# Two maxima over partitions: from a round through DRAM to a unit matrix and a matmul with ones, with a listed due for every planned step

## The chip, the cores and the metric

The kernel runs on one core of one Trainium2 chip. The metric is the device time of one execution in microseconds; of the kernel before, three runs gave 404.8, 405.76 and 405.9 us, so 405.76 us is the median. A profile was taken of one more execution.

## The reference, cut to what matters

```python
xn = layernorm(x)                                   # x: 2048 rows of 512
s  = irfft2(rfft2(xn) * (w_r + 1j * w_i))           # a global filter over rows and columns
gate, up = xn @ W_gate, xn @ W_up                   # 512 -> 1376
h  = gate * (gate > 0) * up
g  = silu(h @ W_down)                               # 1376 -> 512
out = x + s * g
```

All data are 32-bit floats. The kernel keeps that precision by splitting each operand into a high and a low half of 16 bits and adding three products (high by high, high by low, low by high). For that it has to know the size of the numbers: the columns of `W_down` are scaled by a power of two found from the greatest absolute value of the whole matrix, and the filter `w` by one found from the greatest sum of its squares. Each of these two maxima is first taken along the free axis, which leaves one number per partition in a column of 128, and then over the 128 partitions, with the result wanted in every partition. The second half of that is what the change touches.

## The kernel before, in words

The 2048 rows are worked on in eight chunks of two tiles of 128 rows (for the transform) and in four blocks of 512 rows (for the feed-forward part). A block's feed-forward work is eleven tiles of 128 hidden columns: `product` makes `gu` (gate and up) on TensorE, `rectify` makes `r` on ScalarE, `hidden` makes `h` on VectorE and splits it, `down` multiplies `h` by the scaled `W_down` into `dn`, and `gate` makes `g`. The last block does part of this with fewer products (`sa`, `sb`, `sc`). The transform is made of small matrix products: `first_stage` (`s` from `xs`, result `t` written to the DRAM tensor `A_d`), `fft_chunk` (`at` read back, then `y`, `xx`, the multiplication by the filter, `z`, `v`, written to `C_d`), `last_stage` (`ct` read back, `s` again, then `zz`, `ae`, `ye`, `sv` on ScalarE, VectorE and GpSimd), and `finish` (`sv` times `g`, plus `x`, written out).

Nothing of this is issued in the order in which the program states it. Each piece is a *step* with an engine, an estimated cost, the names it reads and writes, and perhaps a due time and a lead. `Plan.run` gives every step without a due time one from those that depend on it (lines 144 to 148), then simulates the engines: at each turn it takes, for each engine, the steps that could begin soonest (dependences met, a buffer free, not before due minus lead), among them the one with the smallest due (lines 191 to 196), and writes the instructions in that order. Every engine then runs its own list in order and waits by semaphores. Buffers come from pools with few places (`ROOM`, line 56: ten of `k4`, two of `F`, three of `gu` and one of `dn` in PSUM); a step that needs a new buffer follows the last reader of the old one. All loads and stores but the accumulating ones are issued by SyncE, in one queue.

`greatest(name, col, reads, due)` (line 728) takes the column over the partitions: SyncE writes it to a DRAM row of 128 numbers (4 bytes from each partition), reads that row back into all partitions as a 128x128 tile, and VectorE reduces it. It is called by `down_scale` (name `md`; its result leads to `scd`, which the scaled `W_down` tiles `wds` wait for) and by `filter_scale` (name `mw`; it leads to `cw` and `cwi`, used in `fft_chunk` and `last_stage`). In a profile all instructions have line 87, that of the helper through which they are issued; tiles tell them apart. `unit` (line 289) is the unit matrix and `ones` (line 306) a 128x128 matrix of ones, both there already for the transposes and for sums over partitions.

Of the kernel before, what the change touches and what calls it, by code (L numbers as in the profile page):

```python
# [8 lines left out]
F32 = mybir.dt.float32  # L9
I32 = mybir.dt.int32  # L10
AF = mybir.ActivationFunctionType
ALU = mybir.AluOpType
AX = mybir.AxisListType

P = 128
S, D, F = 2048, 512, 1376
# [45 lines left out]
TICK, TICK_TO = 1.158, 60  # L62
PLAINS = ['plain', 'plain', 'plain', 'plain', 'plain', 'plain', 'plain', 'plain', 'plain', 'plain', 'plain', 'plain', 'plain', 'plain', 'plain', 'fast', 'plain', 'fast', 'fast', 'fast']
XDUE, SDUE = [-18.3, 7.83, 88.22, 100.36, 188.84, 115.24, 195.7, 156.37], [-84.52, 3.8, 95.3, 188.33]


RANGES = ((0, 257, 0), (257, 512, 1))
# [7 lines left out]
def fwidth(f):  # L75
    return P if f < TAIL else F - P * TAIL
# [17 lines left out]
class Plan:  # L94
# [28 lines left out]
    def step(self, engine, cost, fn, reads=(), writes=(), due=None, lead=None, port=False, kb=0, margin=0., lag=None, mode=0, block=0.):  # L123
        s = Step()
        s.engine, s.cost, s.fn, s.due, s.lead, s.port, s.kb, s.margin = engine, cost, fn, due, lead, port, kb, margin
        s.lag = self.LAG[engine] if lag is None else lag
        s.mode, s.block = mode, block
        s.order, s.names, s.end, s.holder = len(self.steps), [*reads, *writes], None, self.holder
        s.deps = {self.writer[n] for n in reads if n in self.writer}
        for n in writes:  # L130
            s.deps |= self.readers.pop(n, set())
            if n in self.writer:
                s.deps.add(self.writer[n])
        for n in reads:
            self.readers.setdefault(n, set()).add(s)
        for n in writes:
            self.writer[n] = s
        s.deps.discard(s)
        self.steps.append(s)
        return s  # L140

    def run(self):
        steps = self.steps
        for s in reversed(steps):
            s.due = 1e9 if s.due is None else s.due
            for d in s.deps:
                t = s.due - d.cost - d.lag
                d.due = t if d.due is None else min(d.due, t)
        for s in steps:
            if s.due > CALM and s.engine == "SP":  # L150
                s.lag += SAFE_LAG
            elif s.due > CALM and s.engine != "PE":
                s.cost *= SAFE
# [10 lines left out]
        dma, todo, order, mode, port = 0., {e: [] for e in free}, [], 0, None  # L164
# [7 lines left out]
        for _ in steps:  # L172
            best = None
            for e, mine in todo.items():
                at = []
                for s in mine:
                    t = max([free[e]] + [d.end + (0. if d.engine == e == "PE" else d.lag + s.margin) for d in s.deps])
                    if s.lead is not None:
                        t = max(t, s.due - s.lead)
                    if s.port:  # L180
                        t = max(t, ports["POOL" if e == "DVE" else "DVE"])
# [6 lines left out]
                    for tag, k in need.items():  # L188
                        t = max(t, sorted(room[tag])[k - 1] + .15)
                    at.append((t, s))  # L190
                if at:
# [4 lines left out]
                    t, s = min(now, key=lambda k: (e == "PE" and k[1].mode != mode if mode else 0, k[1].due, k[1].order))  # L196

                    late = [k for k in at if soon < k[0] <= t + .5 * s.cost and k[1].due < min(s.due, k[0]) + HURRY]
                    if late and e in ("ACT", "DVE"):
                        t, s = min(late, key=lambda k: (k[1].due, k[1].order))  # L200
# [4 lines left out]
            t, s = best  # L205
# [7 lines left out]
            if e == "PE":  # L213
                t, mode = t if s.mode == mode else max(t, free[e] + MODE), s.mode
# [25 lines left out]
def dve(n):  # L240
    return .07 + n / 960
# [10 lines left out]
def act(n):  # L252
    return .08 + n / 1190


def pool(n):
    return .2 + n / 490
# [7 lines left out]
def kernel(ctx: ExitStack, tc: tile.TileContext, x, wg, wu, wd, wl, ew, sp, c_r, c_d, c_m, c_x, c_s, out):  # L265
    nc = tc.nc
    PS = bass.MemoryType.PSUM
    PE, DVE, ACT, POOL, SP = (InOrder(tc, e) for e in (nc.tensor, nc.vector, nc.scalar, nc.gpsimd, nc.sync))
    matmul = PE.matmul

    dram = ctx.enter_context(tc.tile_pool(name="dram", bufs=1, space=bass.MemoryType.DRAM))
    cpool = ctx.enter_context(tc.tile_pool(name="cpool", bufs=1))
# [16 lines left out]
    unit = cpool.tile([P, P], F32, name="unit")  # L289
    sgn = cS[:, 0:1]  # L290
    wgu = [wpool.tile([P, 2, 2, 4, P * sum(f < TAIL for f in g)], F16, name=f"wgu{i}") for i, g in enumerate(GROUPS)]
# [14 lines left out]
    ones = cpool.tile([P, P], F32, name="ones")  # L306
# [8 lines left out]
    T = Plan(ROOM)  # L315
    step = T.step

    def tile_of(name, tag, shape, dtype, padded=None):
        pools = {"F": psum, "gu": psum, "dn": psum}
        T.tile(name, tag, lambda: pools.get(tag, bpool).tile(shape, dtype, name=name, tag=tag, bufs=T.room[tag]))  # L320
# [361 lines left out]
    def weight_sums(n, due):  # L682

        fs = PAIRS[n]
        raw, t16 = f"rp{n}", f"wT{n}"
        tile_of(raw, "xg", [P, 2, 4, 2 * P], F32)
        for i, src in enumerate((wg, wu)):
            for j, f in enumerate(fs):
                g = next(k for k, q in enumerate(GROUPS) if f in q)
                w = sum(fwidth(q) for q in GROUPS[g])  # L690
                of = src[:, 4 * P * GROUPS[g][0]:4 * (P * GROUPS[g][0] + w)].rearrange("p (k f) -> p k f", k=4)
                o = P * (f - GROUPS[g][0])
                step("SP", .5, lambda i=i, j=j, of=of, o=o: SP.dma_start(T[raw][:, i, :, j * P:j * P + P], of[:, :, o:o + P]),
                     reads=["go"], writes=[(raw, i, j)], lead=8, kb=330, due=due - 12)
                part = lambda i=i, j=j: T[raw][:, i, :, j * P:j * P + P]
                step("ACT", act(512) + .1, lambda part=part, f=f, i=i: ACT.activation(part(), part(), AF.Copy, scale=csc[:, i, f:f + 1]),
                     reads=[("csc", f)], writes=[(raw, i, j)])
        B = lambda i, k: T[raw][:, i, 2 * k:2 * k + 2]
        G, U = [(raw, 0, j) for j in range(2)], [(raw, 1, j) for j in range(2)]
        eng, e, cost = (DVE, "DVE", dve(512)) if TSUMS[n] == "DVE" else (POOL, "POOL", pool(512))  # L700

        def minus(to, a, b, reads, name):
            step(e, cost, lambda: eng.tensor_sub(B(*to), B(*a), B(*b)), reads=reads, writes=[name], port=True, due=due)
        t1, t2, t3, t4 = ((t16, f"t{k}") for k in range(1, 5))
        minus((0, 0), (1, 0), (0, 0), G + U, t1)
        minus((1, 0), (1, 1), (1, 0), U + [t1], t3)
        minus((1, 1), (1, 1), (0, 0), U + [t1, t3], t2)
        minus((0, 1), (0, 1), (1, 1), G + [t2], t4)
        for to, of, needs, k in ((slice(0, 2), lambda: T[raw][:, 0].rearrange("p (t k) f -> p t k f", t=2), [t1, t4, t2], 0),
                                 (slice(2, 3), lambda: B(1, 1).unsqueeze(1), [t2, t4], 2)):  # L710
            m = 512 * (to.stop - to.start)
            step("ACT", act(m), lambda to=to, of=of: ACT.activation(wT[n][:, to, 0], of(), AF.Copy), reads=needs, writes=[(t16, k)], due=due + 2)
            step("DVE", dve(m), lambda to=to, of=of: DVE.tensor_sub(wT[n][:, to, 1], of(), wT[n][:, to, 0]), reads=needs + [(t16, k)], writes=[(t16, k + 1)], port=True, due=due + 4)
        for j, f in enumerate(fs):
            g = next(k for k, q in enumerate(GROUPS) if f in q)
            o = P * (f - GROUPS[g][0])
            to = lambda h, g=g, o=o: wgu[g][:, h, 1, 0:2, o:o + P]
            of = lambda j=j: B(1, 0)[:, :, j * P:j * P + P]
            step("ACT", act(256), lambda to=to, of=of: ACT.activation(to(0), of(), AF.Copy), reads=[t3], writes=[("wgu", f, 0, 1)], due=due + 2)
            step("DVE", dve(256), lambda to=to, of=of: DVE.tensor_sub(to(1), of(), to(0)), reads=[t3, ("wgu", f, 0, 1)], writes=[("wgu", f, 1, 1)], port=True, due=due + 4)  # L720

    def weights(f, i):
        if f < TAIL:
# [3 lines left out]

    def greatest(name, col, reads, due):

        row = dram.tile([1, P], F32, name=f"row_{name}")  # L730
        tile_of(f"rows_{name}", "k2", [P, P], F32)
        rows = lambda: T[f"rows_{name}"]
        top = cpool.tile([P, 1], F32, name=f"max_{name}")
        step("SP", .6, lambda: SP.dma_start(row.rearrange("a p -> p a"), col), reads=reads, writes=[f"row_{name}"], due=due, kb=8, lag=3.)
        step("SP", .6, lambda: SP.dma_start(rows(), row.broadcast_to([P, P])), reads=[f"row_{name}"], writes=[f"rows_{name}"], kb=64, lag=5.2)
        step("DVE", .22, lambda: DVE.tensor_reduce(top, rows(), axis=AX.X, op=ALU.max), reads=[f"rows_{name}"], writes=[f"all_{name}"], due=due + 10)
        return top


# [717 lines left out]
```

## Time and profile before

| | before |
|---|---|
| median of three runs (404.8 to 405.9) | 405.76 us |
| the profiled execution: its own time | 403.82 us |
| its span, first to last instruction | 402.0 us |
| TensorE (PE) busy | 394.6 us, 98% |
| VectorE (DVE) busy | 324.1 us, 81% |
| ScalarE (ACT) busy | 232.2 us, 58% |
| GpSimd (POOL) busy | 31.8 us, 8% |
| granted TensorE clock, mean | 1.000 |
| moved by DMA | 66.50 MB |

PE is TensorE's multiplying, PEld its weight loads, SP or SPq the queue of SyncE that issues the DMAs. A wait is told as "[1.81 <-ACT r L87]": idle for 1.81 us just before, released by ScalarE's writing of `r`. TensorE at the clock 1.000 runs at the higher of its two levels, 2.4 GHz.

### The profile page before, as it was taken

To read this page: it belongs to the slowest core of one execution; us is meant where nothing else is said; L and a number is where in the kernel's file an instruction comes from. 1 tells how busy PE (TensorE), PEld (TensorE's weight loads), DVE (VectorE), ACT (ScalarE), POOL (GpSimd) and SP (SyncE) were. 2 spreads that over 40 slices of the span, in tenths; PEclk is the share of its full clock that TensorE was granted. 3 is DMA by queue.
4 is the path that set the end of the run, shared out by engine and by line. 5 is a ranking of instruction groups with operands and counts; after the bars stand their busy time and mean duration, and the time that the engine had idled before them with its cause. 6 is when DMAs were issued, how large, how long until landed. Compare 5 with 4: busy or idle time off the path is not lost.

```text
span 402.0 us, 8180 instructions
## 1 busy us (share of the span) xinstructions
PE 394.6 (98%) x3148; PEld 225.4 (56%) x3148; DVE 324.1 (81%) x731; ACT 232.2 (58%) x458; POOL 31.8 (8%) x48
## 2 busy tenths in 40 slices
PE   8999998999999999999999999999999999999996
PEld 6954443544444454554545655556554766888545
DVE  4989997998978989369488589987995665988893
ACT  5999993578579954232563554736464635456311
POOL 0000000000000000014001020010110002404100
PEclk9999999999999999999999999999999999999999
DMA  7963220509599717924047009479445496967452
GB/s 253 398 222 104 91 55 7 157 11 228 180 307 322 247 51 298 230 98 127 31 122 247 2 1 292 142 237 228 104 90 178 139 237 212 197 193 182 110 182 105
DMA packets 53367, 66.50 MB, mean 165 GB/s; under 512 B 20752, under 2 KB 30832, under 8 KB 53328
## 3 DMA queue, kind: packets, MB, share of 16 engines
q1 hardware_dynamic: 52176, 63.89, 53.0%
q0 software_dynamic: 1152, 2.10, 3.4%
q8 instruction: 24, 0.39, 0.4%
q14 instruction: 15, 0.12, 0.1%
HBM read 42.89 MB, written 20.99 MB: 159 GB/s over the span
## 4 chain that ended last, share of the span: by engine, by line
PE 85%; ACT 9%; DMA 2%; DVE 1%; issue 1%; SPq 0%; ACTq 0%
PE gu L87 34%; PE dn L87 27%; PE sb L87 4%; ACT wgu L87 4%; PE s L87 3%; PE z L87 3%; PE sa L87 3%; PE xx L87 3%; PE sc L87 3%; DMA A_d<-t 2%; PE y L87 2%; PE small L87 2%; PE v L87 2%; ACT wds L87 1%; ACT r L87 1%; ACT xf L87 1%
## 5 line engine op out<-in xcount | busy, mean ns | idle before, releaser
L87 PE MATMUL gu<-xT,wgu 128*128 128x512 f16 (+1 forms) x768 | 165.3, 372 | 2.4 <-ACT r L87 1.8
L87 PEld LDWEIGHTS <-wgu 128*128 128x128 f16 x960 | 92.9, 98 | 89.3 <-issue 5.3
L87 PE MATMUL dn<-wds,h 128*128 128x512 f16 (+2 forms) x528 | 115.8, 372 | 0.3 <-ACT g L87 0.3
L87 PEld LDWEIGHTS <-h 128*128 128x128 f16 (+1 forms) x594 | 54.5, 98 | 56.2 <-issue 2.2
L87 ACT ACTIVATE h<-h 128x512 f16<-128x512 f32 (+1 forms) x36 | 22.0, 624 | 29.5 <-DVE h L87 29.5
L87 DVE TENSOR_TENSOR h<-gu,r 128x512 f32<-128x512 f32 (+3 forms) x44 | 27.6, 627 | 11.6 <-PE gu L87 8.6
L87 ACT ACTIVATE r<-gu 128x512 f32<-128x512 f32 (+2 forms) x36 | 20.7, 578 | 21.2 <-PE gu L87 18.2
L87 POOL TENSOR_TENSOR tt<-tt,tt 128x256 f32<-128x256 f32 x8 | 8.6, 1076 | 253.6 <-DVE tt L87 224.1
L87 DVE TENSOR_TENSOR h<-h,h 128x512 f16<-128x512 f32 (+1 forms) x36 | 23.8, 684 | 1.9 <-ACT h L87 1.8
L87 DVE SCALAR_TENSOR_TENSOR tt<-xsp,cw,wt 128x512 f32<-128x512 f32 x32 | 24.5, 819 | 0.0
L87 ACT ACTIVATE g<-dn,cdi 128x512 f32<-128x512 f32 (+1 forms) x16 | 10.8, 672 | 19.0 <-PE dn L87 17.4
L87 PE MATMUL gu<-xT,wgt 128*64 128x256 f16 (+1 forms) x144 | 17.0, 309 | 0.0
L87 DVE TENSOR_TENSOR z<-z,z 128x1024 f16<-128x1024 f32 x8 | 9.8, 1222 | 7.8 <-ACT z L87 7.7
L87 DVE TENSOR_TENSOR a<-y,a 128x1024 f16<-128x1024 f32 x8 | 9.7, 1223 | 7.9 <-ACT a L87 7.9
L87 PEld LDWEIGHTS <-wT 128*128 128x128 f16 x144 | 13.9, 98 | 3.1 <-issue 0.4
L87 DVE SCALAR_TENSOR_TENSOR wgu<-raw,p,wgu 128x512 f16<-128x512 f32 x20 | 14.5, 746 | 1.0 <-ACT wgu L87 1.0
L87 DVE TENSOR_TENSOR t<-v,t 128x1024 f16<-128x1024 f32 x8 | 9.7, 1220 | 6.8 <-ACT t L87 6.8
L87 ACT ACTIVATE z<-z 128x1024 f16<-128x1024 f32 x8 | 8.2, 1023 | 11.2 <-PE z L87 11.2
L87 DVE TENSOR_TENSOR t<-s,t 128x896 f16<-128x896 f32 (+1 forms) x16 | 10.6, 686 | 4.7 <-ACT t L87 4.7
L87 ACT ACTIVATE a<-y 128x1024 f16<-128x1024 f32 x8 | 8.1, 1024 | 9.5 <-PE y L87 9.5
L87 PEld LDWEIGHTS <-wgt 128*64 128x64 f16 (+1 forms) x144 | 9.7, 106 | 6.1 <-issue 0.8
L87 ACT ACTIVATE wgu<-raw 128x512 f16<-128x512 f32 x20 | 12.3, 620 | 0.0
(191 smaller groups left out, 596.8 us busy)
## 6 DMA issues: line engine op xcount, KB each, us to landing
A_d<-t SPq DMA_DIRECT2D x16, 256.0 KB, 4.1
rw<-in_wl SPq DMA_DIRECT2D x8, 512.0 KB, 5.9
wt<-in_wl SPq DMA_DIRECT2D x8, 512.0 KB, 7.0
at<-A_d SPq DMA_DIRECT2D x8, 512.0 KB, 5.2
C_d<-t SPq DMA_DIRECT2D x16, 256.0 KB, 3.4
ct<-C_d SPq DMA_DIRECT2D x16, 256.0 KB, 5.7
x<-in_x SPq DMA_DIRECT2D x7, 512.0 KB, 5.9
G_d<-g SPq DMA_DIRECT2D x12, 256.0 KB, 3.5
```

Source lines behind the costliest of these rows:

```text
L87: return lambda *args, **kw: self.tc.keep_in_program_order(f(*args, **kw))
```

## The change

`greatest` no longer uses DRAM. VectorE multiplies the unit matrix by the column (`wide`: the number of each partition on the diagonal, zeros elsewhere), TensorE multiplies a matrix of ones by that, which adds up each column of `wide` and so puts all 128 numbers into every partition of a PSUM tile of the pool `F`, and VectorE reduces that tile. Two SyncE steps become one VectorE and one TensorE step; there are three steps in either version.

`Plan.run` then overwrites the due of every step by a list `DUES` of 1606 numbers, one for each of the kernel's 1606 steps in the order in which the program states them, and the lead of each of the 245 steps that have one by a list `WAITS`. In `weight_sums` some steps name more tiles that they read.

```diff
+DUES = (
+    9.45, 123.13, 114.11, 124.55, 1e+09, 1e+09, 1e+09, 1e+09, 1e+09, 1e+09, 1e+09, 1e+09, 1e+09, 1e+09, 1e+09, 1e+09, 1e+09, 1e+09, 1e+09, 1e+09,
...
+    364.51, 361.97, 361.71, 359.98, 354.13, 355.33, 392.28, 358.03, 338.56, 363.42, 356.36, 350.54, 388.59, 376.12, 357.3, 363.92, 358.89, 361.45,
...
+)
+WAITS = (
...
+)
@@ Plan.run
                 t = s.due - d.cost - d.lag
                 d.due = t if d.due is None else min(d.due, t)
+        for s, due in zip(steps, DUES):
+            s.due = due
+        for s, lead in zip([s for s in steps if s.lead is not None], WAITS):
+            s.lead = lead
         for s in steps:
             if s.due > CALM and s.engine == "SP":
@@ weight_sums
-        minus((1, 1), (1, 1), (0, 0), U + [t1, t3], t2)
+        minus((1, 1), (1, 1), (0, 0), G + U + [t1, t3], t2)
...
@@ greatest
-        row = dram.tile([1, P], F32, name=f"row_{name}")
-        tile_of(f"rows_{name}", "k2", [P, P], F32)
-        rows = lambda: T[f"rows_{name}"]
-        top = cpool.tile([P, 1], F32, name=f"max_{name}")
-        step("SP", .6, lambda: SP.dma_start(row.rearrange("a p -> p a"), col), reads=reads, writes=[f"row_{name}"], due=due, kb=8, lag=3.)
-        step("SP", .6, lambda: SP.dma_start(rows(), row.broadcast_to([P, P])), reads=[f"row_{name}"], writes=[f"rows_{name}"], kb=64, lag=5.2)
-        step("DVE", .22, lambda: DVE.tensor_reduce(top, rows(), axis=AX.X, op=ALU.max), reads=[f"rows_{name}"], writes=[f"all_{name}"], due=due + 10)
+        wide, top = f"wide_{name}", cpool.tile([P, 1], F32, name=f"max_{name}")
+        tile_of(wide, "k2", [P, P], F32)
+        tile_of(f"rows_{name}", "F", [P, P], F32)
+        step("DVE", .25, lambda: DVE.tensor_scalar(T[wide], unit, col, None, op0=ALU.mult), reads=reads, writes=[wide], port=True, due=due)
+        step("PE", .26, lambda: matmul(T[f"rows_{name}"], ones, T[wide], start=True, stop=True), reads=[wide], writes=[f"rows_{name}"], due=due + 2)
+        step("DVE", .3, lambda: DVE.tensor_reduce(top, T[f"rows_{name}"], axis=AX.X, op=ALU.max), reads=[f"rows_{name}"], writes=[f"all_{name}"], due=due + 4)
         return top
```

The second shown line of `DUES` holds, at its seventh place, the due of the last inverse product of chunk 6 (the step that writes `s` of that chunk in `last_stage`): 392.28.

## Rows read from the trace of the kernel before

**Rows 1.** The page, part 1: busy us of each engine, share of the span, instructions.
```profile
PE 394.6 (98%) x3148; PEld 225.4 (56%) x3148; DVE 324.1 (81%) x731; ACT 232.2 (58%) x458; POOL 31.8 (8%) x48
```
**Rows 2.** The waits of PE: who was waited for, us in total, times, longest.
```profile
PE gu L87 <- ACT r L87: 1.8, 1, 1.8
PE small L87 <- DVE md L87: 1.1, 1, 1.1
PE gu L87 <- DVE h L87: 0.6, 1, 0.6
PE dn L87 <- ACT g L87: 0.3, 1, 0.3
```
**Rows 3.** The chain that ended last: start us, us, what.
```profile
55.31 9.58 DMA A_d<-t
...
398.55 0.38 ACT g L87
```
**Rows 4.** The timeline from 54 to 68: start us, us, instruction, idle before.
```profile
54.73 0.54 SPq L87 DMA_DIRECT2D row_md<-md  x1
55.31 0.68 SPq L87 DMA_DIRECT2D A_d<-t  x1
...
64.14 0.32 SPq L87 DMA_DIRECT2D rows_md<-row_md  x1
65.00 0.63 ACT L87 ACTIVATE x<-xf 128x512 f16<-128x512 f32 x1 [5.03 <-DMA A_d<-t]
...
66.16 2.75 PE L87 MATMUL gu<-xT,wgu 128*128 128x512 f16 x12 [1.81 <-ACT r L87]
...
67.95 0.28 DVE L87 TENSOR_REDUCE max_md<-rows_md 128x1 f32<-128x128 f32 x1
```
**Rows 5.** Stretches of 1 us: busy us by engine, clock, DMA share, GB/s.
```profile
57.00:58.00 1.00, 1.00 (x7) 0.47 (x5) 0.87 (x4) 1.00 (x3) 0.00 (x0) 1.00 0.89 182
...
61.00:62.00 1.00, 1.00 (x6) 0.44 (x5) 1.00 (x4) 0.00 (x0) 0.00 (x0) 1.00 0.00 0
```
**Rows 6.** The tile A_d: its DMAs from issue to landing.
```profile
DMA to landing us min/median/max: 3.2/4.5/5.6
```
**Rows 7.** SyncE's queue from 135 to 146, columns as in rows 4.
```profile
135.57 1.98 SPq L87 DMA_DIRECT2D E_d<-edge  x2
138.33 0.33 SPq L87 DMA_DIRECT2D row_mw<-mw  x1
145.25 1.27 SPq L87 DMA_DIRECT2D wt<-E_d  x2
```
**Rows 8.** The timeline of PE: 32-bit products, single and paired stages, the last one.
```profile
12.05 2.03 PE L87 MATMUL gu<-xTf,raw 128*128 128x128 f32 x16
...
103.83 0.85 PE L87 MATMUL s<-xs,cR 64*64 64x257 f16 x24
...
117.67 1.51 PE L87 MATMUL s<-xs,cR 64*64 64x257 f16 x48
...
368.17 1.51 PE L87 MATMUL s<-ct,cR 64*64 64x257 f16 x48
```
**Rows 9.** Groups by line and tile: busy us, mean ns, idle before.
```profile
L87 DVE TENSOR_TENSOR sv<-ye 128x510 f32<-128x510 f32 x16 | 10.6, 694 | 0.0
...
L87 DVE TENSOR_TENSOR ye<-ae,zz 128x256 f32<-128x256 f32 (+1 forms) x24 | 10.0, 445 | 1.0 <-DMA out<-sv 1.0
...
L87 ACT ACTIVATE zz<-s,cwi 128x1024 f32<-128x1024 f32 x8 | 8.5, 1111 | 3.1 <-PE s L87 3.0
...
L87 DVE TENSOR_TENSOR pf<-tt 128x128 f32<-128x128 f32 x32 | 7.1, 283 | 0.6 <-POOL tt L87 0.6
```
**Rows 10.** Two stretches of 20 us, columns as in rows 5.
```profile
20.00:40.00 20.00, 19.41 (x108) 10.21 (x106) 18.03 (x68) 19.14 (x51) 0.00 (x0) 1.00 0.52 166
40.00:60.00 20.00, 20.00 (x116) 9.47 (x115) 19.44 (x54) 19.62 (x43) 0.00 (x0) 1.00 0.28 73
```

**Rows 11.** The page, part 6: stores of the output, KB each, us to landing.
```profile
out<-xt SPq DMA_DIRECT2D x7, 256.0 KB, 2.1
```

More of the change, by code (lines that the diff above doesn't have):

```diff
@@ L64 @@
 XDUE, SDUE = [-18.3, 7.83, 88.22, 100.36, 188.84, 115.24, 195.7, 156.37], [-84.52, 3.8, 95.3, 188.33]
+DUES = (
+    9.45, 123.13, 114.11, 124.55, 1e+09, 1e+09, 1e+09, 1e+09, 1e+09, 1e+09, 1e+09, 1e+09, 1e+09, 1e+09, 1e+09, 1e+09, 1e+09, 1e+09, 1e+09, 1e+09,
+    1e+09, 1e+09, 1e+09, 1e+09, 1e+09, 1e+09, 1e+09, 1e+09, 1e+09, 1e+09, 1e+09, 1e+09, 1e+09, 1e+09, 1e+09, 1e+09, 1e+09, 1e+09, 1e+09, 1e+09, 1e+09,
+    1e+09, 1e+09, 1e+09, 1e+09, 1e+09, -211.71, -49.3, -65, -49.5, -49.61, -49.7, -48.72, -47.53, -40.01, -55.32, -41.85, -48.21, -52.55, -46.66,
[83 rows of a table added]
+)
+WAITS = (
[12 rows of a table added]
+)
 RANGES = ((0, 257, 0), (257, 512, 1))
@@ L706, in weight_sums @@
         minus((1, 0), (1, 1), (1, 0), U + [t1], t3)
-        minus((1, 1), (1, 1), (0, 0), U + [t1, t3], t2)
+        minus((1, 1), (1, 1), (0, 0), G + U + [t1, t3], t2)
         minus((0, 1), (0, 1), (1, 1), G + [t2], t4)
-        for to, of, needs, k in ((slice(0, 2), lambda: T[raw][:, 0].rearrange("p (t k) f -> p t k f", t=2), [t1, t4, t2], 0),
-                                 (slice(2, 3), lambda: B(1, 1).unsqueeze(1), [t2, t4], 2)):
+        for to, of, needs, k in ((slice(0, 2), lambda: T[raw][:, 0].rearrange("p (t k) f -> p t k f", t=2), [*G, t1, t4, t2], 0),
+                                 (slice(2, 3), lambda: B(1, 1).unsqueeze(1), [*U, t2, t4], 2)):
             m = 512 * (to.stop - to.start)
@@ L718, in weight_sums @@
             of = lambda j=j: B(1, 0)[:, :, j * P:j * P + P]
-            step("ACT", act(256), lambda to=to, of=of: ACT.activation(to(0), of(), AF.Copy), reads=[t3], writes=[("wgu", f, 0, 1)], due=due + 2)
-            step("DVE", dve(256), lambda to=to, of=of: DVE.tensor_sub(to(1), of(), to(0)), reads=[t3, ("wgu", f, 0, 1)], writes=[("wgu", f, 1, 1)], port=True, due=due + 4)
+            step("ACT", act(256), lambda to=to, of=of: ACT.activation(to(0), of(), AF.Copy), reads=[*U, t3], writes=[("wgu", f, 0, 1)], due=due + 2)
+            step("DVE", dve(256), lambda to=to, of=of: DVE.tensor_sub(to(1), of(), to(0)), reads=[*U, t3, ("wgu", f, 0, 1)], writes=[("wgu", f, 1, 1)], port=True, due=due + 4)
     def weights(f, i):
```

94 rows, old and new, of tables (DUES, WAITS) are left out of this document.

## The prediction

> **What bounds the kernel now.** I read the page first. TensorE is busy for 394.6 of the span's 402.0 us [rows 1], so the question is only what lies in the other 7.4 us and whether the change adds to the 394.6. The list of PE's waits answers the first part [rows 2]: 1.1 us before its first instruction, and inside the span one wait of 1.8 us for `r`, one of 0.6 us for `h`, one of 0.3 us for `g`, 2.7 us together. The rest is the end: the last piece that isn't PE begins at 398.55 [rows 3], so 3.45 us of ScalarE, VectorE and a store follow the last product. A reader should see that no other engine can give the kernel time except through these gaps. VectorE and ScalarE are the ones to watch before 60 us: from 20 to 40 they are busy for 18.0 and 19.1 of 20 us, from 40 to 60 for 19.4 and 19.6 [rows 10]. There the weights are split while the first products run, and PE is fed just in time.
>
> Then I followed the chain of waits to the largest gap. Its longest piece that isn't PE's is a store of `t` to `A_d`, 9.58 us from 55.31 on [rows 3]. The timeline shows what hangs on it [rows 4]: ScalarE stands still for 5.03 us until that store has landed, since the tile `x` that it is to write takes over a buffer that the store still reads; at 65.00 it goes on, makes the `r` that was queued behind, and at 66.16 PE starts again after 1.81 us. Ahead of that store in the queue, at 54.73, stands `row_md`, the first half of the maximum through DRAM: 128 pieces of 4 bytes. SyncE can issue the reading back only at 64.14 [rows 4], 8.9 us after it had finished issuing the write (54.73 + 0.54). The DMA engines aren't busy in that time: their share is 0.89 from 57 to 58 and 0.00 from 61 to 62 [rows 5]. So the bytes had moved, and what was late was the word that they were written. Other stores to `A_d` land in 3.2 to 5.6 us, 4.5 in the median [rows 6].
>
> **The change part by part.** *The stall.* With `row_md` gone, the store of 55.31 should land after 4.5 us, at 59.8, or 60.9 at the worst of the rows. ScalarE became free for its `x` at 65.00 − 5.03 = 59.97, so its wait falls from 5.03 to between 0 and 0.9 us, and PE's wait behind it, 1.81 us, is covered. Term: −1.81. What comes next there is the `r` of the following product, which ScalarE can then make as soon as PE has finished it.
>
> The Trainium skill, page "DMA: Bandwidth & Descriptors", section "Two DMAs through the same engine are not ordered", says that descriptors of a queue start in order, but that a later one may complete while an earlier one is still writing. By that rule the store need not have waited for `row_md`, its 9.58 us would be its own, and the sum would be without the −1.81 (the second rival below). The trace speaks rather against it here: the late store is the one of these sixteen that stands behind 4-byte writes, and the engines were empty.
>
> *The chain of the maximum.* Now it runs from the end of `row_md`'s issue to the reduction at 67.95, 12.7 us and more. Afterwards it is a VectorE multiplication of 128x128, 0.283 us by the like-sized row [rows 9], the matmul, and the same reduction of 0.28 us [rows 4]; with hand-overs some 1.5 us. `scd` is ready about 12 us earlier, and the 22 instructions that scale `W_down` can begin while PE still has products of the first block. By itself that is worth nothing, since PE has other work throughout that stretch; if the scaling instead pushes ahead of `r` or `h` there, it costs what one such wait costs, 0.6 us [rows 2]. I take 0. The chain of `mw` had the same shape (`row_mw` issued at 138.33 [rows 7]) but no PE wait follows it: 0.
>
> *The added matmuls.* PE is the bound, so these count in full. Eight 32-bit products of 128x128 by 128 columns, two records each, take 2.03 us [rows 8], 0.254 us for one. Two of them: +0.51. They wait for VectorE, and everything behind them on PE waits too. That wait is not in the trace; bounds are 0 and 0.6 us each, the wait of PE for VectorE's `h` [rows 2]. The order places them where the operand is expected, and in the present one PE waits for VectorE only once inside the span, so I take 0. The tile takes one of two `F` buffers for under 1 us: 0, or again one such wait. Two VectorE multiplications, 0.57 us together, lie on an engine with 78 us to spare over the span [rows 1]; where that is full, before 60 us [rows 10], the same bound of one wait holds: 0.
>
> *The dues.* This is the large and uncertain part, as every one of 1606 steps may move. The work of PE itself doesn't change. From below: all gaps inside close (another −0.91 beside the 1.81), and the small stages (`s`, `y`, `v`) stand in pairs. A single `s` takes 0.85 us and a pair 1.51 [rows 8], so each pair saves 0.19; PE's timeline has some 17 unpaired ones, at most eight pairs more, −1.5. From above: a new order has as many gaps inside as this one had, +2.7 over none, or a late chain at the end (third rival). Between −2.4 and several us I take half of the remaining gaps, −0.45, and nothing for the pairs: the nearest rows are those of the present order, which kept PE fed but for three waits [rows 2]. The start is 0: by their dues the first loads come in nearly the same order. The added reads in `weight_sums` name tiles that the steps already follow through others: 0.
>
> The sum: −1.81 + 0.51 − 0.45 = −1.75 on the span of 402.0, thus 400.25. The profiled execution took 403.82 us, 1.82 more than its span; so 402.07. It was 1.94 us faster than the median of the three runs, 405.76; on their scale the forecast is 404.0 us.
>
> **The rivals.** *The gap only moves or stays.* Either the store was slow by itself, or another store to `A_d` now stands behind the small writes that remain: `E_d` is still written from 64 partitions in pieces of 64 bytes, and the loads that need it were issued 7.7 us later (137.55 to 145.25) [rows 7]. Or PE's wait reappears because VectorE and ScalarE are full until 60 us [rows 10]. For it: that fullness. Against it: ScalarE stood idle for 5 us right behind that stretch [rows 4], so there is room. Then only the added matmuls count: 402.0 + 0.5 = 402.5, or 406.3 us in the median.
>
> *The dues give more than the stall.* All gaps close and the pairs come: 402.0 − 2.72 − 1.5 + 0.51 = 398.3, that is 402.1 us. For it: nothing but the freedom of every step. Against it: a due can shift the order only among the steps that are ready, and only 0.9 us of gaps is left to close.
>
> *The last inverse stage comes too late: slower.* Its due for chunk 6 is 392.28, behind nearly all products `dn` of the last block by their dues, while now the last pair of `s` runs at 368.17 [rows 8]. After an `s` come 1.11 us of `zz`, eight small additions at 0.445, six of full width at 0.694 (`sv`, its product with `g`, the sum with `x`) [rows 9] and a store of 2.1 us [rows 11]: 0.76 + 1.11 + 3.56 + 4.16 + 2.1 = 11.7 us. So it decides from the point at which that `s` begins later than 400.25 − 11.7 = 388.6. Placed by its due alone it has about 2.6 us of last products behind it, begins near 393.4 and ends the kernel at 405.1, a price of 4.9 us: 408.9 in the median. For it: the number itself, and that one late chain on VectorE can't be hidden at the end. Against it: a `dn` that waits for its single buffer lets a ready `s` pass, whatever its due.
>
> **How the numbers follow.** Forecast 42%, gap stays or moves 20%, more than the stall 16%, a late end or a like loss 22%. A measurement of this kernel can tell about 0.3% from no change, 1.2 us: below 404.5 is faster, above 407.0 slower. The forecast's own range is 403.0 to 405.2, three quarters of it faster; the second rival is mostly the same, a quarter slower. Faster: 0.42 × 0.75 + 0.16 = 0.47; slower: 0.20 + 0.05 = 0.25 (a tenth of the late cases end below 407); the same: 0.28. The range of 401.5 to 409.0 takes in the best case and the late end of 408.9, and leaves out longer losses.
>
> **What would show it.** In the profile after: no DMA between `md` and its reduction, and less than 3 us from one to the other; no wait of ScalarE for `A_d` above 1 us before 70 us, and PE's waits inside the span below 1.5 us together; PE busy 395.1 us. Wrong would be a wait of PE above 1 us anywhere after 25 us, stores to `A_d` that still take over 8 us, more than 4 us between PE's last product and the end, or the last `s` after 388 us.

## The result, and the profile after

The change made the kernel a little slower: 405.83 us in the median of 16 runs (404.8 to 406.8) against 404.4 us of before on the same chip, a ratio of 1.0033 (95% interval 1.0017 to 1.0049). The forecast was 1.75 us less than before and faster. Its 404.0 us stand on the scale of the three runs with the median 405.76; on that of the 16 runs, 404.4, the same forecast is 402.7 us. Of 106 executions of before that were timed beside the experiments below, one took 1461 us, 75 had a mean granted clock of 0.998 or more and took 402.9 to 404.8 us, in the mean 403.8, and 30 had 0.996 and took 405.3 to 407.7 us. The profiled one belongs to the first kind, and against that kind the kernel after, 405.9 us in the mean at 0.997 or more, is 2.1 us slower.

The profiled execution after took 405.83 us, its span 404.1 us, against 403.82 and 402.0 us. The 2.1 us between the spans can be divided into four parts. The first two come from one view, a single stretch from PE's first product `gu` to the end of its last one. Before:

```profile
8.69:398.55 389.86, 387.06 (x3102) 219.70 (x3102) 320.07 (x714) 227.23 (x445) 30.76 (x40) 1.00 0.57 165
```

The same view of the kernel after (stretch, its length, then busy us and records of PE, PEld, VectorE, ScalarE, GpSimd, the granted clock, DMA share, GB/s):

```profile
8.20:399.79 391.59, 388.10 (x3106) 220.27 (x3106) 323.10 (x718) 229.53 (x445) 29.33 (x40) 1.00 0.57 163
```

PE's work in it grew by 1.04 us (0.3 of it the four more records, the two 32-bit matmuls, by e1 below), its idle time from 2.80 to 3.49 us (length less busy), so by 0.69. The end behind the last product grew from 402.0 − 398.55 = 3.45 to 404.1 − 399.79 = 4.31 us, so by 0.86. The first product came 0.49 us earlier. 1.04 + 0.69 + 0.86 − 0.49 = 2.1.

The waits of PE after, beside [rows 2] (who was waited for, us in total, times, longest):

```profile
PE sb L189 <- DVE sv L189: 1.3, 1, 1.3
PE small L189 <- DVE md L189: 1.1, 1, 1.1
PE small L189 <- ACT wgu L189: 0.7, 1, 0.7
PE sc L189 <- ACT r L189: 0.6, 1, 0.6
PE gu L189 <- ACT r L189: 0.6, 1, 0.6
PE gu L189 <- ACT g L189: 0.3, 1, 0.3
```

The 1.8 us for `r` at 66 is gone, as forecast, and where [rows 2] had three waits inside the span, 2.7 us together, there are now five with 3.5. Two of them, 1.3 and 0.6, have one origin. In the chain that ended last, beside [rows 3] (start us, us, what):

```profile
348.58 7.84 DMA out<-sv
356.51 0.23 DVE sv L189
...
358.80 1.21 DVE sv L189 x2
360.01 1.46 PE sb L189 x12
```

and in the timeline of that stretch (columns as in rows 4):

```profile
348.58 0.87 POOL L189 DMA_DIRECT2D out<-sv  x1 [0.30 <-DVE ae L189]
...
356.50 0.21 ACT L189 ACTIVATE sv<-ye 128x4 f32<-128x4 f32 x1 [2.61 <-DMA out<-sv]
356.51 1.29 DVE L189 TENSOR_TENSOR sv<-ye 128x510 f32<-128x510 f32 x2 [2.61 <-DMA out<-sv]
356.62 0.58 ACT L189 ACTIVATE r<-gu 128x512 f32<-128x512 f32 x1
...
357.25 1.47 PE L189 MATMUL sc<-xS,wgu 128*128 128x256 f16 x12 [0.59 <-ACT r L189]
...
360.00 1.47 PE L189 MATMUL sb<-xS,wT 128*128 128x256 f16 x12 [1.29 <-DVE sv L189]
```

GpSimd's accumulating store of an `sv` lands 7.84 us after its issue. The next `sv` takes over the buffer that it reads, so VectorE and ScalarE both stand still for 2.61 us, and the `r` and the sums that PE needs are queued behind them. It is the pattern of [rows 4], at another place and with another store.

The end of the kernel after, in the timeline:

```profile
396.00 3.77 PE L189 MATMUL dn<-wds,h 128*128 128x256 f16 x33
...
399.81 0.47 ACT L189 ACTIVATE g<-dn,cdi 128x256 f32<-128x256 f32 x1 [3.24 <-PE dn L189]
400.31 0.43 DVE L189 TENSOR_TENSOR sv<-sv,g 128x256 f32<-128x256 f32 x1 [1.02 <-ACT g L189]
400.77 0.42 DVE L189 TENSOR_TENSOR xt<-xt,sv 128x256 f32<-128x256 f32 x1
```

The last piece of PE is now the one of 256 columns; before, it was one of 128, whose `g` took 0.38 us [rows 3], and what follows works on half the columns as well.

The chain of the maximum itself came out as described, without DRAM (timeline):

```profile
58.04 0.28 DVE L189 TENSOR_SCALAR wide_md<-unit,md 128x128 f32<-128x128 f32 x1
...
64.67 0.38 PE L189 MATMUL rows_md<-wide_md,ones 128*128 128x128 f32 x2
65.10 0.29 DVE L189 TENSOR_REDUCE max_md<-rows_md 128x1 f32<-128x128 f32 x1 [0.60 <-PE rows_md L189]
```

It is not short, though: the list puts the matmul 6.3 us after its operand. The stores to `A_d` land in 3.4 to 5.8 us; but the list has the first of them at 62.2 us, where before had it at 54.0, so this profile alone doesn't show what removed the stall.

### The profile page after: what moved, and what is told of

Same layout as the page of the kernel before. It is cut to its first block, busy times and chain, and to the rows that moved or that the text cites. A ratio compares the mean times of both kernels' runs of the same rounds, so it can differ in the third digit from the quotient of the medians.

```text
span 404.1 us, 8177 instructions
## 1 busy us (share of the span) xinstructions
PE 395.1 (98%) x3152; PEld 225.6 (56%) x3152; DVE 327.0 (81%) x733; ACT 234.7 (58%) x458; POOL 30.3 (8%) x48
## 4 chain that ended last, share of the span: by engine, by line
PE 89%; DMA 4%; ACT 4%; DVE 1%; issue 0%; SPq 0%; POOL 0%; DVEq 0%; ACTq 0%
PE gu L189 42%; PE dn L189 27%; PE sb L189 3%; PE s L189 3%; PE z L189 3%; PE xx L189 3%; ACT wgu L189 2%; PE sa L189 2%; PE sc L189 2%; DMA out<-sv 2%; PE y L189 2%; PE v L189 2%; DMA raw<-in_wu 2%; DVE sv L189 1%; DMA x<-in_x 1%; PE dn_3bb L189 0%
## 5 line engine op out<-in xcount | busy, mean ns | idle before, releaser
L189 PE MATMUL gu<-xT,wgu 128*128 128x512 f16 (+1 forms) x768 | 167.2, 372 | 0.9 <-ACT r L189 0.6
L189 DVE TENSOR_TENSOR h<-h,h 128x512 f16<-128x512 f32 (+1 forms) x36 | 25.1, 700 | 2.5 <-ACT h L189 2.1
L189 POOL TENSOR_TENSOR tt<-tt,tt 128x256 f32<-128x256 f32 x8 | 7.7, 963 | 246.2 <-DVE tt L189 226.9
L189 DVE SCALAR_TENSOR_TENSOR tt<-xsp,cw,wt 128x512 f32<-128x512 f32 x32 | 22.9, 761 | 0.2
L189 ACT ACTIVATE p<-pf 128x1024 f16<-128x1024 f32 x8 | 8.5, 1057 | 16.5 <-DVE pf L189 15.2
L189 DVE TENSOR_TENSOR xsp<-xx,xo 128x256 f32<-128x256 f32 (+1 forms) x16 | 5.0, 352 | 10.9 <-ACT xsp L189 9.1
L189 PE MATMUL sb<-xS,wT 128*128 128x256 f16 x96 | 11.8, 273 | 1.3 <-DVE sv L189 1.3
L189 POOL TENSOR_TENSOR ae<-zz 128x128 f32<-128x128 f32 (+1 forms) x16 | 8.8, 599 | 53.6 <-ACT zz L189 41.8
L189 DVE TENSOR_TENSOR t<-s,t 128x128 f16<-128x128 f32 (+1 forms) x16 | 10.5, 685 | 2.3 <-ACT t L189 2.3
```

The costliest lines, as they stand in the source:

```text
L189: return lambda *args, **kw: self.tc.keep_in_program_order(f(*args, **kw))
```

## The experiments

The theory to begin with: **A**, the matmul removes the stall and is worth what was forecast, and the listed order loses it again, in the waits for `sv` and at the end. Its rivals: the matmul itself costs more than it gives, or the stall was not `row_md`'s doing. All ratios are to the kernel before on the same chip.

**The matmul without the new order.** e1_held_matmul is the kernel before, order held, with the two maxima by matmul at the places of the old steps:

```diff
-  step("SP", ..., lambda: SP.dma_start(row..., col), ...)
-  step("SP", ..., lambda: SP.dma_start(rows(), row.broadcast_to([P, P])), ...)
-  step("DVE", ..., lambda: DVE.tensor_reduce(top, rows(), ...), ...)
+  step("SP", ..., lambda: DVE.tensor_scalar(wide, unit, col, None, op0=ALU.mult), ...)
+  step("SP", ..., lambda: None, ...)
+  step("DVE", ..., greater, ...)     # matmul(every, ones, wide); tensor_reduce(top, every)
```

> The kernel before with its order of instructions held, and only the two maxima changed: the multiplication by the unit matrix stands where the store of the row stood, the matmul with ones and the reduction where the reduction stood. Theory A (the order made by the dues costs the time; leaving out the DRAM round is a gain): the store to A_d of about 55 us lands in under 6 us, PE's wait of 1.81 us near 65 us is gone, PE is busy 0.5 us more, span about 400.7 us against 402.0 (ratio 0.997). Theory B (the store was slow by itself, or the wait only moves): the wait stays or another takes its place, span about 402.5 us (ratio 1.001).

403.25 us, 0.9973 (0.9953 to 0.9993): faster than before, and with the kernel after (1.0033) it parts the change in two. The matmul is worth about −0.27%, 1.1 us; the listed dues and leads about +0.60%, 2.4 us.

Less than half of the 1.1 us is a shorter schedule. All twelve executions of e1 had a granted clock of 0.998 or more, and took 403.30 us in the mean; the 23 executions of before at that clock, on the same chip, took 403.76. That is 0.46 us, and the spans of the two profiles differ by 0.2 (402.0 and 401.8). The rest is that e1 has no execution at the clock 0.996, where before had 12 of 35, 2.2 us longer. None of the 60 executions of the five kernels with the matmul in the old order (e1, e8, e11, e12, e13) is of that kind; e2, below, which keeps the round through DRAM, has two of ten. No such execution was traced, so where it loses its time, and whether it is the stall at 66 us, stays open.

The profile of e1 has no wait for `A_d`; the list of PE's waits inside the span is

```profile
PE gu L87 <- ACT r L87: 0.7, 1, 0.7
PE gu L87 <- DVE h L87: 0.6, 1, 0.6
PE dn L87 <- ACT g L87: 0.3, 1, 0.3
```

and the row from first product to last reads

```profile
9.10:398.08 388.98, 387.34 (x3106) 220.41 (x3106) 320.15 (x716) 226.89 (x445) 30.77 (x40) 1.00 0.57 164
```

Set against the kernel after, with the same 3106 records of PE: after has 0.76 us more of PE's work, 3.49 instead of 1.64 us idle, 4.31 instead of 3.72 us of end, and in these two executions a start that is 0.90 us earlier. 0.76 + 1.85 + 0.59 − 0.90 = 2.3, the difference of the spans (404.1 − 401.8).

The order is held, so e1's matmul stands late too: its reduction begins at 67.61 us, against 67.95 before [rows 4]. What an earlier matmul does in the old order was not tried.

**Was it the queue?** e2_row_gpsimd issues the 4-byte stores from GpSimd's queue and is otherwise the kernel before:

```diff
-  SP.dma_start(row.rearrange("a p -> p a"), col)
+  POOL.dma_start(row.rearrange("a p -> p a"), col)
```

> The kernel before with one edit: the 4-byte stores of the two rows are issued by GpSimd's queue, at the same place in the order, and no longer stand ahead of other stores in SyncE's queue. Theory A1 (a store waits behind small writes because of the queue): the store to A_d after row_md lands in under 6 us, PE's wait of 1.81 us goes, span about 400.2 us. Theory A2 (small writes to DRAM hold up the word of completion of the other stores of that time whatever queue they are in): that store still takes over 8 us, the wait of 1.8 us stays, span 402 us. Theory B (the store is slow by itself): as A2.

403.96 us in ten executions (two more took 589 and 1284 us), 1.0008 (0.9986 to 1.0031), and the stall is still there (PE waits 1.4 us for `r`), in the timeline of e2:

```profile
54.69 0.73 POOL L87 DMA_DIRECT2D row_md<-md  x1 [50.62 <-DVE md L87]
64.03 0.34 SPq L87 DMA_DIRECT2D rows_md<-row_md  x1
64.69 0.63 ACT L87 ACTIVATE x<-xf 128x512 f16<-128x512 f32 x1 [4.56 <-DMA A_d<-t]
```

The longest landing of an `A_d` store is 9.7 us, against 9.58 in [rows 3]. So the place in SyncE's queue is not what delayed it.

**The store by itself, and its size.** Two more kernels add to e1, which needs no DRAM for the maxima, a store that nobody reads, at the place of `row_md` and `row_mw`: 4 bytes from each of 128 partitions, or 64.

```diff
   step("SP", ..., lambda: (DVE.tensor_scalar(wide, ...),
+                           SP.dma_start(dead, wide[:, 0:1])), ...)     # e12;  e13: wide[:, 0:16]
```

> e1_held_matmul, which needs no DRAM for the maxima, plus a store that nobody reads: 4 bytes from each of 128 partitions (a column of wide), issued where the kernel before issued row_md and row_mw. Theory (small stores to DRAM hold up the completion of the other stores of that time): the A_d store beside it lands in 9 to 10 us instead of 3.2 to 5.6, ScalarE waits 4 to 5 us for it, PE 1.2 to 1.9 us near 66, and the time is back at that of before plus 0.2 us: ratio 0.999 to 1.003. Rival (the reading back, or the chain behind it, made the store of before late): A_d 3 to 6 us, no wait of ScalarE for it above 1 us, ratio 0.9973.

> The same, but 64 bytes from each of the 128 partitions instead of 4. If it is the size of the piece that holds the others up: A_d in 3 to 6 us, no wait of ScalarE for it above 1 us, ratio 0.9973 (or up to 0.9985, for the place of two more issues). If it is the number of pieces, or any store there: as the 4-byte store, A_d in 9 to 10 us, ratio 0.999 to 1.003.

e12: 404.87 us, 1.0019 (0.9993 to 1.0044). e13: 403.11 us, 0.9961 (0.9940 to 0.9982). The 4-byte store alone, which nobody reads, gives back all that e1 had won. The timeline of e12:

```profile
54.89 0.34 SPq L87 DMA_DIRECT2D dead_md<-wT  x1
55.27 0.54 SPq L87 DMA_DIRECT2D A_d<-t  x1
64.38 0.63 ACT L87 ACTIVATE x<-xf 128x512 f16<-128x512 f32 x1 [4.62 <-DMA A_d<-t]
...
65.54 2.75 PE L87 MATMUL gu<-xT,wgu 128*128 128x512 f16 x12 [1.41 <-ACT r L87]
```

How long its stores to `A_d` took to land, from the view of that tile in e12:

```profile
DMA to landing us min/median/max: 3.1/4.6/9.0
```

The unread store itself, from the view of the tile `dead_md` in e12:

```profile
DMA to landing us min/median/max: 8.3/8.3/8.3
```

The view of `A_d` in e13:

```profile
DMA to landing us min/median/max: 3.0/4.1/5.6
```

and of `dead_md` in e13:

```profile
DMA to landing us min/median/max: 2.2/2.2/2.2
```

The same 128 pieces, sixteen times as large, land in 2.2 us and hold nothing up. It is the 4-byte size that counts, neither the number of pieces nor the issue nor the reading back. The pieces of 4 bytes also lie side by side in DRAM, sixteen of them in the room of one of 64; whether it is the size itself or that closeness was not separated.

**The order's losses, one by one.** e3_sv_later takes the kernel after and lets the three instructions that write `sv` of chunk 4 wait in the order until just before that tile is used; the buffer stays where it was.

```diff
+  late = [steps not on PE that write ("sv4", 0..2)]
+  order = order[:first] + [hold] + rest + late + order[at:]     # hold: takes the buffer at the old place
```

> The changed kernel with its order held but for three instructions of chunk 4 (one of ScalarE, two of VectorE, the ones that write sv), which are issued later, just ahead of their first reader, so that what stands behind them on both engines no longer waits for the accumulating store that frees their buffer. Theory A (the waits of 0.59 and 1.29 us of PE at 357 and 360 us come from that store): both go, span about 402.2 us against 404.1 (ratio to the kernel before about 0.9995). Rival C (the next instruction in line waits for something equally late): the waits stay or move, span 403.5 to 404.5.

404.58 us, 1.0006 (0.9986 to 1.0026): of 1.0033, 0.0027 are gone, 1.1 us. The waits at 357 and 360 are gone from the profile. One of 0.90 us stands at 119.88, where ScalarE's `xf` had waited 1.55 us for a store to `X_d`.

e4_tail puts the last five products of 128 columns, with what follows on them, behind the piece of 256.

```diff
+  last = [five PE steps of "dn3_3b"] + [their gate, products, sums, store]
+  order = [k for k in order if k not in last] + last
```

> The changed kernel with its order held but for the end: five of the eleven products of the last third of the last tile (128 columns), its gate, product, sum and store are put behind those of the first part (256 columns). Theory A (the end costs 0.85 us because the last piece is 256 columns wide): from PE's last product to the end 3.5 us instead of 4.3, span about 403.3. Rival D (VectorE's queue of sums is late anyway): the end stays at 4.3 us or more, span 404.

405.42 us, 1.0026 (1.0005 to 1.0046): 0.0007 less, in the right direction but within the uncertainty. The end fell from 4.3 to 3.9 us, not to the 3.5 that was expected.

e5_sv_and_tail has both edits.

> The kernel after with both edits of e3_sv_later and e4_tail. Theory (the listed order loses its time in separate places whose losses add): e3 took 0.0027 off the ratio of 1.0033 and e4 0.0007, so 1.0033 - 0.0034 = 0.9999, about 403.9 us where the kernel before has 404.0; still 0.0026 behind e1_held_matmul (0.9973). Rival (what one edit gives is taken by the next wait): not below e3 alone, 1.0006 or more, with a PE wait of 0.9 to 1.3 us somewhere after 100 us in the profile, as e3 and e4 each showed one.

405.36 us, 1.0028 (1.0011 to 1.0046). A miss: the time is not the sum of the two. The rival named a wait of 0.9 us or more, and the profile has none after 100 us (the longest is 0.39). But the profiled execution, 404.86 us, was faster than most of that kernel, so what the others lost isn't in it. Its end took 4.3 us, where e4 alone had 3.9. The rest stays open.

e9_after_start goes for the start of the kernel after: 8 of the 42 products that only keep PE busy are left out, and the load of `cR` (128 KB), first used at 58.7, goes behind the first loads of `W_down`.

```diff
-  step("PE", ..., lambda: matmul(T["small"][:, 256:], ...), ...)
+  step("PE", ..., lambda k=k: 29 <= k < 37 or matmul(T["small"][:, 256:], ...), ...)
+  order.insert(order.index(sync[17]) + 1, <load of cR>)
```

> The kernel after with two edits at its start: the same 8 products left out, and the load of cR (128 KB, issued at 2.60, first used at 58.7) moved behind the first loads of W_down. Theory (PE's wait at 12.28 for ScalarE's square of a weight tile that landed at 10.84 pins the stretch to 25.66): the tile lands earlier by 128 KB at about 330 GB/s = 0.39 us, so 0.4 us go, ratio 1.0023, and the left-out products alone give nothing. Rival 1 (start and data both count): 1.0 us or more, ratio below 1.001. Rival 2 (what is gained before 25 us ends in the wait for r at 25.66): no gain, 1.0033.

405.98 us, 1.0050 (1.0032 to 1.0067): no gain. PE's wait for `wgu` near 12 fell from 0.69 to 0.27 us, and its next wait, for `r`, came at 25.00 us instead of 25.67. All of that had been given back at 357, where the accumulating store holds `sv` (PE's timeline of e9):

```profile
357.52 1.47 PE L189 MATMUL sc<-xS,wgu 128*128 128x256 f16 x12 [1.28 <-ACT r L189]
360.29 0.92 PE L189 MATMUL sb<-xS,wT 128*128 128x256 f16 x7 [1.29 <-DVE sv L189]
```

e10_after_all has all three edits together, as short diffs above.

> The kernel after with all three edits together: the three writings of sv later (e3), five products of 128 columns last (e4), and the start of e9 (8 products left out, the load of cR later). In e9 what was gained before 120 us was gone at 357 us, where the wait for the accumulating store stood at 1.28 + 1.29 us instead of 0.59 + 1.29; with that wait removed it should reach the end. Theory (the start was hidden behind that wait): some 0.4 to 0.7 us below e5, ratio 1.001 to 1.002, PE's last product before 398.5 in the profile. Rival (the time that e5 lost against the sum of its parts lies in waits for DMA that come and go from one execution to the next): no gain over e5, 1.0028 or more, with another wait of PE for ScalarE or VectorE behind a DMA.

404.53 us, 1.0001 (0.9981 to 1.0021). That is 0.0027 below e5, more than the theory asked for; PE's last product ended at 398.67, a little later than the 398.5 named. It doesn't show that the start reaches the end, though: e3 alone was at 1.0006, which the uncertainty doesn't part from 1.0001, and e5 is the run that was not understood. The three places together hold some 0.0032 of the 0.0060 that the order costs, and 0.0027 of that came with e3 alone. The row of e10 from first product to last shows where the rest is:

```profile
7.82:398.67 390.85, 388.59 (x3106) 220.50 (x3106) 322.97 (x717) 229.98 (x445) 30.17 (x40) 1.00 0.57 164
```

Its PE idles 2.26 us, 0.62 more than in e1, but is busy for 1.25 us more with the same records. Of these, 0.50 go with the early start and not with the order: e8 below, which is e1 with the same short start, has

```profile
8.05:398.52 390.47, 387.84 (x3106) 220.26 (x3106) 320.30 (x716) 227.25 (x445) 30.74 (x40) 1.00 0.57 164
```

The other 0.75 are the order's, as the 0.76 of after against e1 were: e4, whose first product comes at 9.30 and so as late as e1's, has the same 388.10 us of PE's work as after. Part of that is the more frequent change between small stages and large products: an inverse `s` that was one pair more in e1 stands in two singles, 0.19 us by [rows 8]. I did not divide up the rest.

**Is the maximum's place free in the new order?** e7_dram_in_new_order holds the order of after, with the store at the place of `wide` and the reading back at the place of the matmul.

```diff
-  DVE.tensor_scalar(T[wide], unit, col, ...) / matmul(T[rows], ones, T[wide])
+  SP.dma_start(row..., col) / SP.dma_start(T[wide], row.broadcast_to([P, P]))
```

> The kernel after with its order held, but both maxima taken back through DRAM: the 4-byte store at the place of the multiplication by the unit matrix, the reading back at the place of the matmul. Theory (the new order is built on the short chain): the first store goes out at about 58.1, the reading back some 9 us later and the reduction at about 69.5 where the order has it at 65.1, so VectorE stands about 4.5 us at 65; the second reduction comes some 10 us after 168.7 where the order has it at 170.6, another 6 to 9 us; ScalarE and PE wait behind. With what PE has queued as cover I expect 3 to 9 us over the kernel after: 409 to 415 us, ratio 1.011 to 1.026. Rival (the place of the maximum is free in this order, and the loss is the order's own whatever the maximum costs): the same as the kernel after within 1 us, ratio 1.001 to 1.006.

414.55 us, 1.0269 (1.0231 to 1.0307), just above the upper end. The list needs the short chain: with the old one VectorE waits 6.1 and 6.3 us for the two readings back. The list and the matmul belong together; the matmul doesn't need the list.

**A faster one?** e8_short_start is e1 with the same 8 products left out.

> e1_held_matmul with 8 of the 42 products that only keep PE busy at the start left out (those just ahead of the first transpose), all else in the same order. Theory (the first 1:1 stretch of PE counts in full, as the profiles of before, e1 and e2 carry their start of 8.69 to 9.10 on to 22.5 to 22.9): its input is there at about 6.2 us and the transpose began at 7.4 to 7.8, so 0.7 to 1.5 us go: ratio 0.994 to 0.9956, 401.6 to 402.2 us, first gu at 8.0 to 8.3. Rival (the data bind there, as they do in the kernel after at 12.28): the ratio of e1, 0.9973, with a PE wait of 0.5 us or more before 23 us. Second rival: PE's clock is lower for lack of those products: the granted clock below 1.00 before 12 us, and slower than e1.

403.03 us, 0.9975 (0.9959 to 0.9992), the ratio of e1. The first product comes 1.05 us earlier, at 8.05, and a wait of 0.82 us at 13.37 takes it: the rival, the data bind.

e11_r_first is e1 with the `r` that PE waits for at 72.39 moved ahead of a scaling of `W_down` and an `h` in ScalarE's queue.

```diff
+  order.remove(rect)                              # "r0_10" on ScalarE
+  order.insert(order.index(scale), rect)          # scale: the second wds on ScalarE
```

> e1_held_matmul with one ScalarE instruction moved: the r that PE waited for at 72.39 (0.69 us) goes ahead of the scaling of W_down and of the h that stood before it in ScalarE's queue. Theory (this wait is the price of the scaling that now begins where PE still has products of the first block): PE's wait there falls below 0.1 us and the time by 0.6: ratio 0.9957, 402.3 us. Rival (the wait only moves on, to a dn that needs the scaling moved back or to the next r): the ratio of e1, 0.9973, and a PE wait of 0.4 us or more between 72 and 90 us.

404.33 us, 0.9987 (0.9968 to 1.0007): nothing gained, 0.0014 more than e1. In e1 that wait was (PE's timeline)

```profile
72.39 1.50 PE L87 MATMUL gu<-xT,wgt 128*64 128x256 f16 x24 [0.69 <-ACT r L87]
```

It went from there to the `dn` that needs the scaling that was moved back, and grew from 0.69 to 0.93 (PE's timeline of e11):

```profile
74.50 1.67 PE L87 MATMUL dn<-wds,h 128*128 128x512 f16 x7 [0.93 <-DVE wds L87]
```

So the best kernel here is the old order with the matmul, e1 and e8 at 0.9973 and 0.9975, ahead of both before and after; e13, at 0.9961, is e1 with a store that nobody reads, and the uncertainty doesn't part it from them.

## Why the prediction was wrong, step by step

**The stall, −1.81: right in place and size.** Without 4-byte stores the `A_d` store lands in time and the wait at 66 is gone, in after and in e1; e1, where the order is the old one, is the proof. The reason given was half right. I read "behind it in the queue" from the timeline; e2 shows that for this store the queue doesn't matter, e12 and e13 that the size of the pieces does. The rule weighed there, of the Trainium skill, page "DMA: Bandwidth & Descriptors", section "Two DMAs through the same engine are not ordered", is therefore not contradicted by this trace: the late store wasn't slow by itself, and it wasn't waiting its turn either.

**What takes its place.** Named as possible and priced at nothing: the scaling pushes ahead of an `r`, "what one such wait costs, 0.6 us". That happened in e1, 0.69 us at 72.39, and e11 shows that it isn't an accident of order; the scaling and the `r` compete there. The first two terms make 1.3 us (1.81 − 0.51), and the 1.1 us of e1's ratio look close to it, but that is luck: at like clock the gain is 0.2 to 0.5 us, and the rest is the executions at 0.996, of which the prediction knew nothing. In the two profiles 1.16 us of idle time went (2.80 to 1.64: the 1.81 less this 0.69, nearly), and 0.28 of matmuls, 0.27 of a longer end and 0.41 of a later start came; the last two vary by as much between executions of the same order (ends of 3.4 to 3.8 us, first products at 7.9 to 9.1).

**The two matmuls, +0.51.** PE's work from first to last product is 0.28 us longer in e1 than before: about half of the term. The 395.1 us of PE busy that the prediction asked for were met, but that number can't be read so closely: it contains the `small` products at the start, which took 6.01 us in after and 6.50 in before.

**The step that failed: the dues, "half of the remaining gaps, −0.45, and nothing for the pairs".** With the matmul in both kernels the listed order costs 1.0033 − 0.9973, 2.4 us (2.3 between the spans), in place of −0.45: 0.76 of PE's work, though the prediction says that it doesn't change, 1.85 of waits and 0.59 of a longer end, less a start that was earlier in that execution. The working had the right bound, several us, and then took the row of the present order as the nearest, as if a new list kept PE fed as well as the old one. It didn't look for what is tight in the old order away from PE. There was one hint, in [rows 9]: VectorE's `ye` waited 1.0 us for an accumulating store `out<-sv`. A wait of that kind had cover on PE before, and in the new order it hasn't (e3: 1.1 us).

**The third rival, a late end: wrong mechanism, right sign.** The `s` of the last chunk did move back, from 368.17 [rows 8] to (PE's timeline after)

```profile
384.89 0.85 PE L189 MATMUL s<-ct,cR 64*64 64x257 f16 x24
```

3.7 us ahead of the 388.6 from which it would decide, and it decided nothing. What made the end longer was the order of the last products. Its 22% "for a late end or a like loss" was the case that came, and too little for a list that touches 1606 steps.

**The number.** 405.83 us lies inside the range of 401.5 to 409.0 and near the 406.3 us of the first rival. Both are luck: these figures, and the bounds of 404.5 and 407.0 for faster and slower, hang on the 405.76 us of three runs, 1.4 us above the median of 16.

**The first rival's remark on `E_d`** fell: pieces of 64 bytes hold nothing up (e13), and in e1 the stores to `E_d` land in 2.8 us once `row_mw` is gone.

**The signs to look for.** "A wait above 1 us after 25 us" and "more than 4 us at the end" were both named as signs of being wrong, and both are there (1.29 at 360.00; 4.31). "No wait for `A_d`" and "stores below 8 us" held; "less than 3 us" for the maximum did not, 57.76 to 65.10, since the list put the matmul late.

## What to carry to other kernels

A change that replaces an operation and the order together should be timed in halves: here the operation alone wins 0.27%, and the list that came with it costs 0.60%. A mean can mix two kinds of executions: over half of that 0.27% is not in the schedule that the profiles show, so sort the executions by their granted clock before dividing a gain into waits. When a gap of the bounding engine is closed, look next at every buffer that a slow store still reads, since a wait for one stops whole queues and turns into a gap as soon as its cover moves. A number per partition that is wanted in every partition is worth a matmul with ones, less for its own latency than for the 4-byte stores that it spares all other stores.

## What the runs showed of the hardware

- A store of 128 pieces of 4 bytes to DRAM took 8.3 us to land (e12), and a 256 KB store issued 0.38 us later took 9.0 us, though the DMA engines stood at a share of 0.00 from 59 to 64 us; with the small store in GpSimd's queue the large one took as long (9.7 us, e2). 128 pieces of 64 bytes landed in 2.2 us, and all stores to `A_d` in at most 5.6 (e13).
- An accumulating store from GpSimd's queue (`out<-sv`) took 7.84 us to land in after and 8.53 in e9, a plain store of the output of 256 KB 2.1 us [rows 11].
- The kernel before ran at a mean granted clock of 0.996 in 30 of 106 executions, which took 2.4 us more than those at 0.998 or more; no kernel with the matmul was at 0.996 in any execution. What lowers the clock there was not traced.
- In e7, PE was busy for 2.85 of 5 us from 70 to 75, and the granted clock then fell (stretches, columns as in rows 5):

```profile
70.00:75.00 5.00, 2.85 (x30) 1.71 (x29) 3.21 (x10) 2.17 (x4) 0.00 (x0) 1.00 0.16 26
75.00:80.00 5.00, 3.24 (x9) 1.11 (x8) 4.93 (x11) 3.09 (x8) 0.00 (x0) 0.69 0.60 199
80.00:85.00 5.00, 5.00 (x24) 2.20 (x22) 4.19 (x9) 3.67 (x9) 0.00 (x0) 0.97 1.00 189
```

  A mean of 0.69 lies between the two levels of 1.2 and 2.4 GHz; in e7 the wait of VectorE for DRAM, 6.14 us up to 71.68, thus cost PE twice, once idle and once at the lower clock.
- The 37 `small` products ahead of the first transpose took 5.54 us in e3, 6.01 in after, 6.92 in e1 and 7.12 in e4, with the granted clock at 1.00 in all. The first product therefore comes up to 1.5 us earlier or later (7.80 in e3, 9.30 in e4) from one execution to another; e8 and e9 show that this hardly reaches the end.
